# Row masks on VectorE, the gate's weights earlier in the load queue, early rows turned inside the last attention step, and w2 loaded in halves

## The chip, the cores and the metric

The kernel runs on one core of a Trainium2 chip. The metric is the device time of one execution in microseconds. Smaller is better.

A core has these engines: PE (TensorE, matrix products and transposes by a unit matrix), DVE (VectorE), ACT (ScalarE), POOL (GpSimd) and SP (SyncE, which here only starts transfers). Each takes its instructions in the order of the program, so one that waits holds up all that stand behind it on the same engine. Matrix products are written to PSUM, and DVE or ACT carry them on to SBUF.

## What is computed

A recurrent attention, then a mixture of experts on its output, all in float32.

```python
# retention: B=4, H=8 heads, S=768 steps, D=64; gamma depends on the head
for t in range(S):
    state = gamma * state + outer(k[:, :, t], v[:, :, t])
    y[:, :, t] = (q[:, :, t] @ state) / sqrt(D)
x = y.transpose(0, 2, 1, 3).reshape(3072, 512)      # one row per token
# experts: E=8, hidden width F=1024
logits = x @ w_gate                                  # (3072, 8)
expert = argmax(logits, axis=1)
gate   = softmax(logits)[row, expert]
for e in range(E):
    rows = (expert == e)
    out[rows] = gate[rows] * (relu(x[rows] @ w1[e]) @ w2[e])
```

## The kernel before, in words

**Attention.** The 768 positions are cut into 6 chunks of 128, and the work into 12 steps (STEPS). A step handles one chunk of two of the four batches. The order of instructions on every engine is the order of the program: a manual schedule covers all engines from line 738 on. A step s does the following.

- SP starts the loads of k and v three steps ahead, in odd steps those of q too (lines 762 to 766). SP's queue is one line: the loads, then the stores of finished rows (`store`, line 586), then the weights of the first expert. The loads of steps 0 to 2 are started before the loop (lines 727 to 737), and the load of the gate's weights `wg` follows them (line 739).
- POOL scales q and v by the decay (`scale_q`, `scale_v`, lines 473 and 481).
- PE makes the scores (`scores`, 513), whose causal mask DVE applies (line 523, tile `am`); adds the part that comes from the state (`with_state`, 534); multiplies the output of the step before by the gate's weights (`logits`, 595, tile `parts`); turns the next step's k and, in odd steps, q (`turn_k`, `turn_q`, tiles `trk` and `trq`); transposes the logits back (`logits_of`, 606); makes the next state (`next_state`, 544, tile `new`); and makes the output inside the chunk (`within`, 562, tile `y`), in two halves of the heads. ACT and DVE copy `y` to the tile `xT`.
- DVE turns `xT` to rows (`to_rows`, 580, tile `xg`), and SP stores them in device memory (`x_d`).

PSUM is handed out by tags: four banks "sc" (scores, `parts`, early products `hp`), two "tr" (`trk`, `new`, `rk`, `found`, `tre`), two "y". A tile waits until the bank it takes over has been read out.

**Routing.** `place(i)` (line 616) is a generator that is advanced in pieces. It places the tokens of steps 0 to 4 (i = 0), 5 to 8 (i = 1) and 9 to 11 (i = 2). Its pieces: the one-hot choice of an expert and the gate (627 to 652; POOL splits the gate in three bfloat16 parts, `told`, for i > 0); the rank of each token within its expert by small products `rk` (654 to 667); a mask `here` per tile of 128 tokens, which says in which row a token goes (`find`, 679 to 682: one instruction per tile, on DVE for i = 0 and on POOL for i > 0); the values `val` (692); the product `found` of both (699), and its addition to `inv`, the table from places to tokens (705). For i = 1 the rows of the first 256 tokens of experts 0 and 1 are then fetched from `x_d` by indirect transfers that POOL starts (`gather`, 709). A table `WHEN` (755) says at which points of steps 5 to 10 a piece is advanced: "p" is ahead of `logits`, "a" after the stores, "b" after `next_state`, "r" ahead of `within`, "c" after it.

**The early job.** After the last step, expert 0's first 256 rows (EARLY) are computed while the last tokens are placed: `xe` (821) brings the fetched rows into head order, PE turns them (`tre`, 833) to `xTa`, and eight rounds of `layer1` (tile `hp`, 843) make the hidden layer `hTa`. Between the rounds stand the pieces of `place(2)`: `rk` after round 1, `found` and `inv` after round 4. The second layer is done by `pair` (345) with seven half-size products instead of eight. They need sums of quarters of w2 (`halves_of_w`, 263, tiles `we`) and of the hidden layer (`halves_of_h`, 252, tiles `he`). Lines 850 to 872 set the order: `sources` (from places to tokens), gathers, gates, `arms` (sizes of the experts), the four `we` (0, 1, 3 on DVE, 2 on POOL), the four `he`, then `pair`, the turning of the late rows on DVE (213), and `targets` (187: eight small DVE instructions, which give the rows of the output).

**The eight jobs.** Then each expert has one job (from line 984) of two layers, with the rest of expert 0 first. DVE turns the rows of the next job, POOL makes the sums of the weights, SP loads weights two jobs ahead.

Of the kernel before, what the change touches and what calls it, by code (L numbers as in the profile page):

```python
# [53 lines left out]
def kernel(  # L54
# [99 lines left out]
            nc.sync.dma_start(w1t[:, :, :, part], w1v[:, ds(e, 1), :, part])  # L154
        return w1t

    def weights2(pool, e):
        w2t = pool.tile([P, 1, FT, DM], F32, tag="w2t", name="w2t")
        nc.sync.dma_start(w2t, w2v[:, ds(e, 1), :, :])
        return w2t  # L160

    def weights(pool, e):
# [89 lines left out]
    def halves_of_h(hT, hs, others=nc.vector):  # L252


        hs = [h.rearrange("p (f t) -> p f t", f=FH) for h in hs]
        a11, a12, a21, a22 = (hT[:, ts(j, FH), ts(i, P)] for i in range(2) for j in range(2))
        nc.vector.tensor_tensor(out=hs[0], in0=a21, in1=a22, op=ALU.add)
        nc.vector.tensor_tensor(out=hs[1], in0=hs[0], in1=a11, op=ALU.subtract)
        others.tensor_tensor(out=hs[3], in0=a12, in1=hs[1], op=ALU.subtract)
        others.tensor_tensor(out=hs[2], in0=a11, in1=a21, op=ALU.subtract)  # L260
        return hs

    def halves_of_w(w2t, ws, which=range(4), by=nc.vector):
# [176 lines left out]
    with ExitStack() as actx:  # L440
# [87 lines left out]
        def outputs():  # L528
            return [ps("y", 2, "y").rearrange("p (b a t) -> p b a t", b=2, a=HB) for _ in range(2)]
# [29 lines left out]
            else:  # L559
                nc.vector.tensor_tensor(out=state[b1], in0=new, in1=old, op=ALU.add)  # L560

        def within(s, y, am):
            alone = 2 * where[s][0] + where[s][2] == 0
            x[s] = keep.tile([P, DT, 2, P], F32, tag="xT", name="xT", bufs=2)
            for half in range(2):
                for b in range(2):
                    vs = raw["vs", s, b]
                    for a in range(half * HB, (half + 1) * HB):
                        for j in ((1, 0) if half else (0, 1)):
                            nc.tensor.matmul(place_of(y, b, a, j), lhsT=vs[:, 2 * a + j, :], rhs=am[b][j][:, a, :],  # L570
                                             start=alone, stop=True, skip_group_check=True)
            nc.scalar.copy(out=x[s][:, 0:HB, :, :].rearrange("p a b t -> p b a t"), in_=y[0])
            for j in range(2):
                to, got = x[s][ts(j, D), HB:HP, :, :].rearrange("p a b t -> p b a t"), y[1][ts(1 - j, D), :, :, :]
                if j and s + 1 == STEPS:
                    nc.vector.tensor_copy(to, got)
                else:
                    nc.scalar.copy(out=to, in_=got)

        def to_rows(s):  # L580
            xg = x["g", s] = keep.tile([P, 2, Q, DT * L], F32, tag="xg", name="xg", bufs=3)
# [34 lines left out]
        def place(i):  # L616
# [61 lines left out]

            def find():
                for b in range(n):  # L680
                    by.tensor_scalar(out=here[:, b, :], in0=rrow, scalar1=prow[:, b : b + 1], scalar2=None,
                                     op0=ALU.is_equal)

            if i:
                find()
            else:
                yield
                tell()
                yield
# [4 lines left out]
                ap=[list(at_f.ap[0]), list(at_f.ap[1]), [0, 5], list(at_f.ap[2])]))  # L694
            if i == 0:
                yield
                find()
            yield
            found = ps("tr", 2, "found")[:, 0 : 5 * E * TC]
            for b in range(n):  # L700
# [22 lines left out]
        def load_all(nm, s):  # L723
            for b in range(2):
                load(nm, s, b)
# [2 lines left out]
        load("k", 0, 0)  # L728
        load("q", 0, 1)
        load("k", 0, 1)  # L730
        load_all("v", 0)
        load_all("k", 1)
        load_all("v", 1)
# [2 lines left out]
        load_all("k", 2)  # L736
        load_all("v", 2)
        ctx.enter_context(tc.manual_schedule(engines={PE, ACT, POOL, DVE, SP}))
        nc.sync.dma_start(wg[:, :, 0:E], w_gate.rearrange("(dt p) e -> p dt e", p=P))
        xTa = first.tile([P, DT, EARLY], F32, tag="xTa", name="xTa")  # L740
        xT1 = first.tile([P, DT, W], F32, tag="xT1", name="xT1")
        hTa = keep.tile([P, FT, EARLY], F32, tag="hTa", name="hTa")
# [8 lines left out]
        turn_k(0, 1)  # L751
        am.append(scores(0, 1))
        xe = keep.tile([P, HALF, DM], F32, tag="xe", name="xe")
        rest = iter(())
        WHEN = {5: "abc", 6: "ab", 7: "ab", 8: "pa", 9: "ar", 10: "pp"}

        def step(s, at):
            for _ in range(WHEN.get(s, "").count(at)):
# [2 lines left out]
        for s in range(STEPS):  # L761
            if s + 3 < STEPS:
                if s % 2:
                    load_all("q", s + 3)
                load_all("k", s + 3)
                load_all("v", s + 3)
            if s % 2 and s + 1 < STEPS:
                scale_q(s + 1, 1)
            if s + 1 < STEPS:
                for b in range(2):  # L770
                    scale_v(s + 1, b)
            if s % 2 == 0 and s + 2 < STEPS:
                scale_q(s + 2, 0)
            if s in (1, 2):
                nc.gpsimd.memset(xs2[s % 2], 0.0)
            if s:
                am = [scores(s, b) for b in range(2)]
            y = outputs()
            if where[s][0] or where[s][2]:
                with_state(s, y)  # L780

            def ahead():
                for b in range(2):
                    turn_k(s + 1, b)

            def ahead_q():
                if s % 2:
                    for b in range(2):
                        turn_q(s + 1, b)

            step(s, "p")
            if s:
                logit = logits(s - 1)
                if s + 1 < STEPS:
                    ahead()
                reduce = logits_of(s - 1, *logit)
                if s + 1 < STEPS:
                    ahead_q()
                to_rows(s - 1)
                reduce()  # L800
                store(s - 1)
                if s == NEXT[NR - 1]:
                    wa = [weights1(first, 0, 2)]
                if s + 1 == STEPS:
                    wa.append(weights2(first, 0))
                if s in NEXT:
                    rest = chain(rest, place(NEXT.index(s) - 1))
                step(s, "a")
            next_state(s)
            step(s, "b")  # L810
            if s == NEXT[NR - 1] + 1:
                pad_ranks(acc[:, NR - 1, 0:2])
            step(s, "r")
            within(s, y, am)
            if s == 0:
                ahead()
            step(s, "c")

        for t in range(HALF):
            copy = nc.scalar.copy if t else nc.vector.tensor_copy  # L820
            copy(out=xe[:, t, :].rearrange("p (a q l) -> p q a l", q=Q, l=L),
                 in_=xs2[0][:, t, :].rearrange("p (q a l) -> p q a l", q=Q, l=L))
        logit = logits(STEPS - 1)
# [6 lines left out]
        for t in range(HALF):  # L830
            tr = ps("tr", 2, "tre").rearrange("p (a t) -> p a t", a=DT)
            for dt in range(DT):
                nc.tensor.transpose(tr[:, dt, :], xe[:, t, ts(dt, P)], ident)
            if t:
                nc.scalar.copy(out=xTa[:, :, ts(t, P)], in_=tr)
            else:
                nc.vector.tensor_copy(xTa[:, :, ts(t, P)], tr)
        logits_of(STEPS - 1, *logit)()
        next(rest)
        to_rows(STEPS - 1)  # L840
        store(STEPS - 1)
        for f in range(FT):
            layer1(EARLY, xTa, wa[0], hTa, f, (("sc", 4),))
            if f == 1:
                next(rest)
                ne = count()
            if f == 4:
                next(rest)
                next(rest, None)
        src, far = sources(inv, "")  # L850
# [229 lines left out]
```

## Time and profile before

| | |
|---|---|
| median of three runs (and the three) | 470.91 us (471.14, 470.91, 466.03) |
| the profiled execution's own time | 469.96 us |
| its span, first to last instruction | 468.2 us, so 1.76 us lie around it |
| attention steps, early job, jobs | from 0 to 129, to 165, to the end (us in the span) |
| mean granted TensorE clock | 0.978 |
| bytes moved | 72.77 MB, mean 155 GB/s |

How to read the profile. The page gives busy time per engine, then the span in 40 slices. The chain of waits follows the work that ended last back to what released it. A timeline line has start and length in us, the engine, the line of the code, the operation, the tiles (out<-in) and a count; the brackets hold the idle time ahead of it and what ended it. "SPq" is the queue that starts transfers: a long entry there is an instruction that could not hand over its transfer sooner. "PEld" is the loading of a matrix operand, which overlaps the products. Windows give busy time per engine in a stretch, the granted TensorE clock (1.00 is full speed), the share of the transfer engines' time and the rate.

### The profile page before, as it was taken

The numbers are of one execution on the slowest core, as the hardware profiler recorded it, in microseconds if no ns is written. First come the engines' busy times: TensorE is split into PE (matmuls) and PEld (weight loads), VectorE is DVE, ScalarE is ACT, GpSimd is POOL, SyncE is SP. The second block draws the span as 40 slices with busy tenths as digits, with TensorE's granted clock in tenths as the row PEclk, the third lists the DMA queues.
The fourth block names the chain that finished last, engine by engine and source line by source line (L and its number), as shares of the span: only waits on it lengthen the run. The fifth ranks groups of instructions, "written<-read, shape, count | busy, mean of one in ns | idle before, by whom it ended". The sixth has DMA issues, their size and how long they took to land.

```text
span 468.2 us, 9505 instructions
## 1 busy us (share of the span) xinstructions
PE 437.6 (93%) x3595; PEld 358.8 (77%) x3595; DVE 277.4 (59%) x571; ACT 125.2 (27%) x284; POOL 258.0 (55%) x217
## 2 busy tenths in 40 slices
PE   7779999998887999999999999999989999999992
PEld 5668888786675884558987995898889599699772
DVE  4416469957558693942676567358756748744410
ACT  2334563552322020221231122114212212212310
POOL 4548535518246137819833891886389189179311
PEclk9979999998999799999999999999999999999998
DMA  8999999996671079705804441380472416001001
GB/s 200 226 238 208 236 228 227 227 228 207 165 237 41 3 256 383 293 4 208 285 3 183 156 168 50 138 299 22 182 227 91 174 44 223 5 6 63 4 28 49
DMA packets 94457, 72.77 MB, mean 155 GB/s; under 512 B 53883, under 2 KB 78459, under 8 KB 94337
## 3 DMA queue, kind: packets, MB, share of 16 engines
q1 hardware_dynamic: 89072, 58.74, 43.9%
q0 software_dynamic: 5120, 12.60, 7.6%
q8 instruction: 48, 0.79, 0.7%
q14 instruction: 73, 0.59, 0.4%
q10 hardware_dynamic: 144, 0.05, 0.0%
HBM read 60.88 MB, written 14.68 MB: 161 GB/s over the span
## 4 chain that ended last, share of the span: by engine, by line
PE 78%; DVE 7%; DMA 4%; SPq 3%; issue 2%; POOL 2%; ACT 1%; POOLq 0%; DVEq 0%; ACTq 0%
PE p L307 24%; PE p L353 18%; PE p L240 13%; PE p L227 5%; PE y L570 3%; PE sc L521 3%; DMA q<-in_q_dram 3%; DVE xT L213 2%; SPq L470 2%; PE new L554 2%; PE trk L489 2%; PE hp L227 2%; PE yp L353 1%; PE y L541 1%; PE parts L600 1%
## 5 line engine op out<-in xcount | busy, mean ns | idle before, releaser
L240 PE MATMUL p<-w2t,hT 128*8 128x128 f32 (+6 forms) x496 | 66.7, 362 | 0.0
L240 PEld LDWEIGHTS p<-w2t,hT 128*8 128x8 f32 (+6 forms) x496 | 32.2, 122 | 30.2 <-issue 26.7
L213 DVE STREAM_TRANSPOSE xT<-xs 32x512 f32<-32x512 f32 x64 | 44.9, 702 | 6.3 <-issue 5.2
L398 POOL DMA_INDIRECT out_dram<-o,dst x30 | 29.9, 995 | 28.2 <-ACT o L248 11.8
L483 POOL TENSOR_TENSOR vs<-v,dec 128x512 f32<-128x512 f32 x23 | 23.6, 1046 | 38.3 <-PE y L570 33.9
L523 DVE TENSOR_TENSOR am<-sc,causal 128x512 f32<-128x512 f32 x48 | 29.9, 681 | 21.6 <-PE sc L521 21.6
L1039 POOL COPY turn_of<-t 128x1 f32<-128x1 f32 x6 | 1.1, 184 | 73.6 <-DVE t L293 73.6
L213 DVE STREAM_TRANSPOSE xTs<-xs 32x512 f32<-32x512 f32 x48 | 33.7, 702 | 11.9 <-issue 11.1
L353 PE MATMUL p<-ws,hs 128*128 128x256 f32 x168 | 37.4, 379 | 0.0
L170 POOL DMA_INDIRECT xs<-x_d,src x28 | 28.5, 1016 | 14.3 <-issue 7.9
L307 PE MATMUL p<-t,s 128*128 128x196 f32 (+5 forms) x192 | 35.8, 329 | 0.0
L307 PE MATMUL p<-t,w1t 128*128 128x196 f32 (+5 forms) x192 | 35.8, 329 | 0.0
L311 DVE TENSOR_TENSOR hT<-p,q 128x196 f32<-128x196 f32 (+5 forms) x72 | 23.8, 359 | 19.4 <-PE p L307 18.5
L353 PEld LDWEIGHTS p<-ws,hs 128*128 128x128 f32 x168 | 31.9, 190 | 4.3
L269 POOL TENSOR_TENSOR ws<-w2t,ws 128x1024 f32<-128x1024 f32 x14 | 33.1, 2363 | 0.5
L269 POOL TENSOR_TENSOR ws<-w2t 128x1024 f32<-128x1024 f32 x14 | 33.1, 2364 | 0.1
L307 PEld LDWEIGHTS p<-t,s 128*128 128x128 f32 x192 | 32.4, 190 | 0.0
L307 PEld LDWEIGHTS p<-t,w1t 128*128 128x128 f32 x192 | 32.4, 190 | 0.0
L359 DVE SCALAR_TENSOR_TENSOR o<-p,gate,q 128x256 f32<-128x256 f32 x21 | 10.1, 483 | 30.9 <-PE p L353 30.4
L521 PE MATMUL sc<-qT,kT 64*128 64x128 f32 x384 | 25.6, 280 | 2.5 <-ACT kT L508 2.3
L478 POOL TENSOR_TENSOR qs<-q,dec 128x512 f32<-128x512 f32 x22 | 22.4, 1045 | 9.6 <-DMA q<-in_q_dram 9.6
L311 DVE TENSOR_TENSOR q<-p,q 128x196 f32<-128x196 f32 (+5 forms) x48 | 16.3, 360 | 19.0 <-PE p L307 14.4
(211 smaller groups left out, 842.9 us busy)
## 6 DMA issues: line engine op xcount, KB each, us to landing
w2t<-in_moe_w_dram SPq DMA_DIRECT2D x8, 2048.0 KB
w1t<-in_moe_w_dram SPq DMA_DIRECT2D x7, 2048.0 KB, 8.2
k<-in_k_dram SPq DMA_DIRECT2D x24, 256.0 KB, 5.2
v<-in_v_dram SPq DMA_DIRECT2D x24, 256.0 KB, 4.7
x_d<-xg SPq DMA_DIRECT2D x48, 128.0 KB, 3.7
q<-in_q_dram SPq DMA_DIRECT2D x11, 512.0 KB, 6.7
w1t<-in_moe_w_dram SPq DMA_DIRECT2D x2, 1024.0 KB
q<-in_q_dram SPq DMA_DIRECT2D x2, 256.0 KB, 3.5
```

Of the source, the lines that this page charges most:

```text
L170: nc.gpsimd.indirect_dma_start(out=xs[:, t, :], out_offset=None, in_=x_d[0:rows, :], in_offset=bass.IndirectOffsetOnAxis(ap=idx[:, t : t + ...
L213: nc.vector.transpose(xT[ts(g, L), :, 0 : n * P].rearrange("p a (t r i) -> p r t a i", r=Q, i=L)[:, r, :, :, :], xs[ts(r, L), tiles[0] : t ...
L227: nc.tensor.matmul(hp, lhsT=w1t[:, 0, dt, ts(f, P)], rhs=xT[:, dt, 0:n], start=(dt == 0), stop=(dt == DT - 1))
L240: nc.tensor.matmul(y[j * z : j * z + m, 0:c], lhsT=hT[:, f, t * P + r0 : t * P + r0 + m], rhs=w2t[:, 0, f, ts(j, c)], start=(i == 0), stop ...
L269: by.tensor_tensor(out=ws[i], in0=sums[i][0], in1=sums[i][1], op=ALU.subtract)
L307: nc.tensor.matmul(rows(y), lhsT=a(d, f), rhs=b(d), start=start and d == 0, stop=d == 1, skip_group_check=True)
L311: nc.vector.tensor_tensor(out=to, in0=rows(y), in1=rows(plus), op=ALU.add)
L353: nc.tensor.matmul(y, lhsT=a[:, f, :], rhs=b[:, f, :], start=start and f == 0, stop=f == FH - 1, skip_group_check=True)
L398: done = nc.gpsimd.indirect_dma_start(out=out[:, :], out_offset=bass.IndirectOffsetOnAxis(ap=idx[:, t : t + 1], axis=0), in_=o[:, t, :], i ...
L483: by.tensor_tensor(out=vs, in0=raw.pop(("v", s, b)), op=ALU.mult, in1=inner(dec[:, ts(NC + 2 * where[s][0] + where[s][2], H)], D))
L521: nc.tensor.matmul(sc[j][:, a, :], lhsT=kT[r, a, :], rhs=qT[r, a, :], start=True, stop=True)
L523: nc.vector.tensor_tensor(out=am[j], in0=sc[j], in1=middle(causal[:, :], HP), op=ALU.mult)
```

## The change

Six edits are made at once:

1. `find` always runs on DVE, after `val`; so the masks `here` of `place(1)` (8 instructions) and `place(2)` (6) go from POOL to DVE.
2. The load of `wg` stands ahead of the loads of v in SP's queue. In the built program it comes right after the first of the two loads of v for step 0.
3. In `WHEN`, step 8 has "pp" in place of "pa": the addition to `inv` of `place(0)` stands ahead of `logits`, the turning of k and `to_rows`.
4. In the last step, `logits` of the step before stands ahead of `with_state`; ACT makes both `xe`; PE turns the early rows between the two halves of `within`, and the copy of the first half of `y` follows that half (in every step). The copy of the second half is on ACT alone.
5. The logits of the last step come after round 0 of `layer1`, their reduction, the first piece of `place(2)`, `to_rows` and the stores after round 1, `rk` after round 3, `count` after round 4, `found` and `inv` after round 6. w2 of expert 0 is loaded in two halves of 1 MB: the first where the whole was, the second behind the last stores.
6. `targets` of the main table is done ahead of the sums `we`; the fourth `we` stands after the `he`; in `halves_of_h` the third sum is made before the fourth (in the jobs too).

```diff
-    def weights2(pool, e):
-        w2t = pool.tile([P, 1, FT, DM], F32, tag="w2t", name="w2t")
-        nc.sync.dma_start(w2t, w2v[:, ds(e, 1), :, :])
+    def weights2(pool, e, part=range(FT), w2t=None):
+        if w2t is None:
+            w2t = pool.tile([P, 1, FT, DM], F32, tag="w2t", name="w2t")
+        part = slice(part.start, part.stop)
+        nc.sync.dma_start(w2t[:, :, part, :], w2v[:, ds(e, 1), part, :])
...
+        others.tensor_tensor(out=hs[2], in0=a11, in1=a21, op=ALU.subtract)
         others.tensor_tensor(out=hs[3], in0=a12, in1=hs[1], op=ALU.subtract)
-        others.tensor_tensor(out=hs[2], in0=a11, in1=a21, op=ALU.subtract)
...
-        def within(s, y, am):
+        def within(s, y, am, between=lambda: None):
...
             for half in range(2):
+                if half:
+                    between()
...
-            nc.scalar.copy(out=x[s][:, 0:HB, :, :].rearrange("p a b t -> p b a t"), in_=y[0])
+                if not half:
+                    nc.scalar.copy(out=x[s][:, 0:HB, :, :].rearrange("p a b t -> p b a t"), in_=y[0])
...
-                if j and s + 1 == STEPS:
-                    nc.vector.tensor_copy(to, got)
-                else:
-                    nc.scalar.copy(out=to, in_=got)
+                nc.scalar.copy(out=to, in_=got)
...
-                    by.tensor_scalar(out=here[:, b, :], in0=rrow, scalar1=prow[:, b : b + 1], scalar2=None,
+                    nc.vector.tensor_scalar(out=here[:, b, :], in0=rrow, scalar1=prow[:, b : b + 1], scalar2=None,
                                      op0=ALU.is_equal)
-            if i:
-                find()
-            else:
+            if i == 0:
...
             if i == 0:
                 yield
-                find()
+            find()
...
         load("k", 0, 1)
+        nc.sync.dma_start(wg[:, :, 0:E], w_gate.rearrange("(dt p) e -> p dt e", p=P))
         load_all("v", 0)
...
-        nc.sync.dma_start(wg[:, :, 0:E], w_gate.rearrange("(dt p) e -> p dt e", p=P))
...
+        def early_rows():
+            for t in range(HALF):
+                copy = nc.scalar.copy if t else nc.vector.tensor_copy
+                tr = ps("tr", 2, "tre").rearrange("p (a t) -> p a t", a=DT)
+                for dt in range(DT):
+                    nc.tensor.transpose(tr[:, dt, :], xe[:, t, ts(dt, P)], ident)
+                copy(out=xTa[:, :, ts(t, P)], in_=tr)
...
-        WHEN = {5: "abc", 6: "ab", 7: "ab", 8: "pa", 9: "ar", 10: "pp"}
+        WHEN = {5: "abc", 6: "ab", 7: "ab", 8: "pp", 9: "ar", 10: "pp"}
...
             y = outputs()
+            if s + 1 == STEPS:
+                logit = logits(s - 1)
             if where[s][0] or where[s][2]:
                 with_state(s, y)
...
+                if s + 1 == STEPS:
+                    for t in range(HALF):
+                        nc.scalar.copy(out=xe[:, t, :].rearrange("p (a q l) -> p q a l", q=Q, l=L),
+                                       in_=xs2[0][:, t, :].rearrange("p (q a l) -> p q a l", q=Q, l=L))
                 reduce = logits_of(s - 1, *logit)
...
-                    wa.append(weights2(first, 0))
+                    wa.append(weights2(first, 0, range(FT // 2)))
...
-            within(s, y, am)
+            within(s, y, am, early_rows if s + 1 == STEPS else lambda: None)
...
         for f in range(FT):
             layer1(EARLY, xTa, wa[0], hTa, f, (("sc", 4),))
+            if f == 0:
+                logit = logits(STEPS - 1)
             if f == 1:
+                logits_of(STEPS - 1, *logit)()
                 next(rest)
+                to_rows(STEPS - 1)
+                store(STEPS - 1)
+                weights2(first, 0, range(FT // 2, FT), wa[1])
+            if f == 3:
+                next(rest)
+            if f == 4:
                 ne = count()
-            if f == 4:
+            if f == 6:
                 next(rest)
                 next(rest, None)
...
         arm, over = arms(ne)
+        dst = targets(inv, far, "")
         halves_of_w(wa[1], we, [0, 1])
         halves_of_w(wa[1], we, [2], nc.gpsimd)
+        S = halves_of_h(hTa, [att.tile([P, FH * P], F32, tag="k", name="he", bufs=8) for _ in range(4)], nc.gpsimd)
         T = halves_of_w(wa[1], we, [3])
-        S = halves_of_h(hTa, [att.tile([P, FH * P], F32, tag="k", name="he", bufs=8) for _ in range(4)], nc.gpsimd)
...
         turn(xs2[1], xT1, range(TC))
-        dst = targets(inv, far, "")
```

More of the change, by code (lines that the diff above doesn't have):

```diff
@@ L792 @@
             if s:
-                logit = logits(s - 1)
                 if s + 1 < STEPS:
+                    logit = logits(s - 1)
                     ahead()
+                if s + 1 == STEPS:
+                    for t in range(HALF):
+                        nc.scalar.copy(out=xe[:, t, :].rearrange("p (a q l) -> p q a l", q=Q, l=L),
+                                       in_=xs2[0][:, t, :].rearrange("p (q a l) -> p q a l", q=Q, l=L))
                 reduce = logits_of(s - 1, *logit)
@@ L817 @@
             step(s, "c")
[L819 to L823, printed above, removed]
         rest = place(NR - 1)
@@ L827 @@
               for tag, bufs in [("q", 4)] * 4]
[L830 to L841, printed above, removed]
         for f in range(FT):
             layer1(EARLY, xTa, wa[0], hTa, f, (("sc", 4),))
+            if f == 0:
+                logit = logits(STEPS - 1)
             if f == 1:
+                logits_of(STEPS - 1, *logit)()
                 next(rest)
+                to_rows(STEPS - 1)
[4 more added lines that the diff above has]
+            if f == 4:
                 ne = count()
-            if f == 4:
+            if f == 6:
                 next(rest)
```

## The prediction

> **What bounds the kernel now.** I read the page first, then what PE waited for, then the chain of waits, then timelines around each break.
>
> ```profile
> PE 437.6 (93%) x3595; PEld 358.8 (77%) x3595; DVE 277.4 (59%) x571; ACT 125.2 (27%) x284; POOL 258.0 (55%) x217
> ...
> PEclk9979999998999799999999999999999999999998
> DMA  8999999996671079705804441380472416001001
> ```
>
> PE is the bound nearly everywhere, and from 180 us on (the jobs) it has hardly a gap. The change must earn its time before that. There PEclk has three dips (slices of 11.7 us), and the transfer engines are full until about 105 us. What PE waited for up to 180 us, longest total first (total, times, longest):
>
> ```profile
> PE parts L600 <- DMA wg<-in_moe_w_gate_dram: 4.6, 1, 4.6
> PE yp L353 <- DVE he L258: 3.5, 1, 3.5
> ...
> PE found L701 <- POOL here L681: 2.0, 6, 0.3
> ```
>
> The chain (start, length) has the same three places:
>
> ```profile
> 20.44 1.64 POOL qs L478 x2
> ...
> 22.75 3.71 DMA wg<-in_moe_w_gate_dram
> 26.47 0.14 issue
> 26.60 1.08 PE parts L600 x8
> 27.68 1.90 PE trk L489 x8
> 29.58 0.43 PE parts L609 x2
> 30.01 2.48 PE trq L489 x16
> 32.49 1.08 PE new L554 x32
> ```
>
> PE stood from 22.0 to 26.6 for the gate's weights. What follows is slow as well: the clock is halved (windows of four us; PEclk is third from the right).
>
> ```profile
> 24.00:28.00 4.00, 1.40 (x10) 0.61 (x11) 0.00 (x0) 0.26 (x1) 3.15 (x4) 0.57 1.04 217
> 28.00:32.00 4.00, 4.00 (x24) 4.00 (x23) 0.23 (x1) 2.26 (x5) 1.16 (x1) 0.58 1.10 239
> ```
>
> Two timeline lines matter for DVE and POOL together: an addition of two SBUF tiles on DVE that takes 0.69 us elsewhere took 2.83 us beside POOL's sum, and ended 0.55 us after it.
>
> ```profile
> 147.65 2.43 POOL L269 TENSOR_TENSOR we<-w2t 128x1024 f32<-128x1024 f32 x1
> 147.80 2.83 DVE L257 TENSOR_TENSOR he<-hTa 128x512 f32<-128x512 f32 x1
> ```
>
> [...] clock 0.50 from 24.6 to 31.3, 113.4 to 116.4 and 150.9 to 157.4 us, each after 2.6 to 4.4 us of little work. [...] k and v move in 256 B pieces; the trace has 229 GB/s here (40 to 104 us) and 390 GB/s for the experts' weights.
>
> **Part by part,** gains counted positive, in the base of the times above.
>
> *wg early.* Its transfer is issued 17 us sooner, so the stall goes. The loads behind it slip by its own slot: an SP entry of 1.00 us, but 16 KB; I take 0.5. PE is free at 21.97. Next it needs k (last issue ended 20.07) and POOL's fourth product of q, which ended at 24.48, now 24.98. At full clock `parts`, `trk`, `parts`, `trq` take 0.57+1.02+0.22+1.75 (rows of the step at 45 us). If only q holds, the last quarter of `trq` (0.44) follows at 24.98, and `new` starts at 25.5. If k lands 5 us after its issue ended (v's time to landing is 4.9), 25.1+0.22+1.75 gives about 27.5 with gaps. I take 26.4 against 32.41: **+6.0** (4.9 to 6.9).
>
> *Does it last to step 9?* The SP queue is never free until 105 us, so the loads keep their times; PE alone moves up. The narrow places: q of step 8 was scaled by 75.33 and is turned at 81.92; q of step 10 by 93.16, turned at 101.4; the last k of step 8 lands by about 74 (issue plus 4.6), turned at 81.1. Shifts of 6.0 to 7.2 leave 0.6 to 1.2 us. It lasts, barely.
>
> *Step 8, inv ahead.* `found` holds one of the two "tr" banks until `inv`, which ran at 93.48, behind `to_rows` and the logits; so the second `trk` waited 0.73 and `new` 0.60. Now `inv` follows `am` (end 91.38) and ends at 91.7: `trk` 91.75, `parts`, `new` at 92.65 instead of 93.84: **+1.2** (0 to 1.2).
>
> *Step 10, here on DVE.* Now POOL's eight masks (0.60 us apart, with a lock by `val` 5.65 in all) hold `found` until 112.53. On DVE one takes 0.24 us alone, 0.17 from start to start, as step 7's first ones did; 8 make 1.4. `val` ends at 108.1, masks at 109.5, then the four `am` that stand behind them on DVE; `parts` needs the first `am`'s bank: 110.25 instead of 112.46. The second `trk` waits for `inv` behind `am` (112.4). `new` starts at 113.25 and takes 1.15 instead of 1.84, [...]. `within` at 114.4 instead of 117.03: **+2.6**. The lower bound: POOL's two products for v of step 11 (1.04 each) stood behind the masks and now are free. If they fall on `val` and the masks, DVE loses 2.1 us, the clock falls, and the part gives -0.6. Their v is issued at 98.03 and 98.95 and lands at about 102.6 and 103.6; shifted by 7.2, the masks end at 102.3. So +2.6.
>
> *Last step.* From `within` of step 10 to that of step 11 is 7.7 us: scores 2.93, of which 0.87 is gaps, `with_state` 1.40, a wait of 0.55 for `lgT`. With `parts` ahead that wait is covered: 6.4: **+1.3** (0.4 to 1.9).
>
> *Early rows.* From `within` to the first `hp` now 5.7 us. Then: half 0.95, `tre` 1.1, half 0.9: 2.9: **+2.8**. It needs `xe` in time: ACT makes it during `with_state` if the gathered rows are there (rivals).
>
> *Given back before inv.* From first `hp` to the end of `inv`: 11.0 us now, five rounds of 1.8 plus 2. Afterwards seven rounds (12.6), `parts` 0.6, transposes 0.3, `rk` 0.3, `found` 0.6, `inv` 0.35: 14.8: **-3.8**. DVE's chain (masks ready 0.05 after round 5) and the second half of w2 (behind the stores; lands 4 us before it is needed) are hidden under these rounds. `place(2)`'s masks on DVE cost nothing: POOL ended them at 139.9, PE asked at 140.5.
>
> *From inv to he.* PE's stall of 3.5 us is on DVE: 9.92 us from `inv` to the second `he`. Out goes the fourth `we` (1.27), in come eight `targets` (1.45, 178.26 to 179.71). POOL's `we` still locks the first `he`; POOL's own `he` no longer waits for DVE's, so it may lock the second (1.26). Between 10.3 and 11.5: **-0.9** (-0.4 to -1.6).
>
> *The tail.* `targets` ended at 179.7; PE waited 0.55 for it before job 1. Job 0 ends at 179.13 and the turned rows at 178.23: **+0.5**.
>
> *Nothing:* the swapped order of sums in the jobs; both are ready before the third product, and if not, 0.69 us per job.
>
> Sum: 6.0+1.2+2.6+1.3+2.8-3.8-0.9+0.5 = +9.7. From the profiled execution (span 468.2, 1.76 around it, 469.96): span 458.5, **460.3 us**. The median of the runs shown is 0.95 higher.
>
> **Rivals.**
>
> *The loads take over* (0.20). Leads of 0.6 to 1.2 us rest on landing times that I could only bound. If k or q comes 3 us late, PE stops at `trk` or `trq` in steps 7 to 10: 3+0+1.5 for the first three parts, +4.4 in all: 465.6. For it: transfer share 0.9 to 1.1 throughout. Against: PE waited for no k in steps 2 to 11.
>
> *The lock and the clock* (0.14). v of step 11 lands early, [...] the third part is -0.6: 463.4. Decides whether the vs products start before the masks end.
>
> *More* (0.07). DVE is past its first `he` when POOL's `we` begins, and PE's rest before `yp` gets short enough for full clock: 24 products took 8.46 us where 24x0.237 = 5.7 would do. About +14: 456.
>
> *Slower* (0.05). PE's `tre` now stands inside the last step, and the second half of `within`, `hp` and all behind it queue there. It needs `xe`, that needs the gather, that needs step 8's stores to have landed, which SP's queue keeps at about 108.3 (issue to 104.94, plus 3.7). The second gather would start at 109.6; `tre` is due at 114.1. Each us of delay costs one; from a landing at 123.8 on the kernel is slower. The trace only shows that rows whose second issue began at 116.52 were there by 127.25; the same 10.7 gives 120.3. I put it at 471.5.
>
> *As forecast* (0.54).
>
> **How the numbers follow.** 2% is about what a measurement of this kernel can tell from no change; it is 461.5 us against the median. The forecast case spreads by some 1.5 us, so about 0.8 of it is past 2%, with the case "more" and a little of the lock's 0.52; slower by over 2% 0.04; within 0.44. The range 455.5 to 467.0 leaves out half of "slower" and the ends of the first and third rival. The forecast's own range is 458 to 463.
>
> **What would show it.** Right: no wait for wg, clock 1.00 from 24 to 32, `new` of step 1 at 26 to 27; no POOL masks; PE's gap before `parts` of step 10 under 2 us with clock 1.00 after it; first `hp` near 116; `inv` near 131; still a wait of `yp` for `he`, now longer than 3.5. Wrong: PE waits for k, q or qs between 35 and 105; `val` or `here` on DVE with lengths of 1 us or more; a wait of `tre` for `xe`; `found` late after round 6.

## The result, and the profile after

The changed kernel takes 463.75 us (median of 18 runs, 460.40 to 466.17), the kernel before 467.69 us (18 runs beside it, 464.38 to 472.94). The ratio is 0.991 with a 95% interval of 0.9884 to 0.9937: 4.2 us less, between 2.9 and 5.4. By 2% that counts as the same. The forecast was 460.3 with a range of 455.5 to 467.0. (The ratios leave out runs that lie over 1.5% above the fastest of their kernel, so they can differ from the ratio of two medians.)

The two profiled executions stand 9.5 us apart (span 468.2 and 458.7), nearly the forecast sum of 9.7. That agreement is partly luck: the profiled execution of the changed kernel is the fastest of its 18, and 1.65 of the 9.5 us arise behind the start of job 1, where the change has no term. Finding out how much is luck was the main work of the experiments. The page of the changed kernel has, for the busy row and the clock and transfer rows that the prediction showed of before:

```profile
PE 432.3 (94%) x3595; PEld 352.8 (77%) x3595; DVE 278.8 (61%) x583; ACT 126.1 (27%) x286; POOL 249.1 (54%) x203
...
PEclk9999999999995999999999999999999999999998
DMA  9999999999750099425614713281481524001001
```

The dips of PEclk in the third and the tenth slice are gone, and one is left at 140 us, where VectorE makes the `he`. What PE waited for up to 180 us (total, times, longest):

```profile
PE yp L355 <- DVE he L260: 4.9, 1, 4.9
...
PE yp L355 <- DVE bt L196: 2.0, 1, 2.0
...
PE rk L657 <- DVE ohs L636: 1.5, 1, 1.5
PE trk L491 <- DMA k<-in_k_dram: 1.4, 2, 0.9
```

`wg` has left the list, and `found <- POOL here` with it. In their place stand `rk` for DVE (0.2 before), `trk` for the landing of k and `yp` for `bt` (neither in the list of before). The last costs nothing: it ends at 136.7 us, and eight products later PE waits for `he` until 144.2 in any case. The wait for `he` has grown by 1.4. The chain (start, length) from 18 us on shows what holds PE where `wg` did:

```profile
17.71 5.98 DMA k<-in_k_dram
...
23.73 0.66 PE trk L491 x4
...
24.61 1.75 PE trq L491 x16
26.35 1.08 PE new L556 x32
```

and the windows over the same eight microseconds, which ran at 0.57 and 0.58 of the clock before, are now at full clock (PEclk is third from the right):

```profile
24.00:28.00 4.00, 4.00 (x68) 3.83 (x68) 0.74 (x2) 2.79 (x5) 3.14 (x3) 1.00 1.08 231
28.00:32.00 4.00, 4.00 (x65) 3.28 (x62) 1.87 (x4) 1.85 (x4) 2.42 (x3) 1.00 0.96 235
```

The next table follows the path through the timelines. Later experiments left the code up to some point untouched, so that one piece of code was traced several times; the columns "all" give those traces, the first one included (`tail_only`, which stands in two rows of before, differs there in the order of the copies of `y`).

| start of (us) | before | before, all | changed | changed, all |
|---|---|---|---|---|
| `new`, step 1 | 32.42 | 30.9 to 32.4 (3) | 26.29 | 26.2 to 26.7 (11) |
| `new`, step 8 | 93.84 | 92.3 to 93.8 (3) | 86.47 | 86.4 to 88.9 (8) |
| `new`, step 10 | 115.15 | 114.3 to 115.2 (3) | 106.14 | 106.1 to 109.3 (8) |
| first `hp` | 130.44 | 129.7, 130.4 | 118.75 | 118.5 to 121.6 (8) |
| end of last `inv` | 141.44 | 140.7, 141.4 | 133.24 | 133.2 to 135.9 (5) |
| job 0 | 164.98 | 162.1, 165.0 | 157.29 | 157.3 to 159.9 (4) |
| job 1 | 179.68 | 179.7 | 171.78 | 171.8, 174.7 |
| end | 468.2 | 468.2 | 458.7 | 458.7, 464.5 |

The traced execution of the changed kernel is near the early end of its kind at every mark, and that of the kernel before near the late end. By the means of these few traces the gain is 10.0 us at the first `hp` (130.1 against 120.1) and 5.3 at job 0 (163.5 against 158.2), where the profiled pair has 11.7 and 7.7.

### The profile page after: what moved, and what is told of

Read it like the earlier page. It is cut to its first block, busy times and chain, and to the rows that moved or that the text cites. A ratio compares the mean times of both kernels' runs of the same rounds, so it can differ in the third digit from the quotient of the medians.

```text
span 458.7 us, 9508 instructions
## 1 busy us (share of the span) xinstructions
PE 432.3 (94%) x3595; PEld 352.8 (77%) x3595; DVE 278.8 (61%) x583; ACT 126.1 (27%) x286; POOL 249.1 (54%) x203
## 4 chain that ended last, share of the span: by engine, by line
PE 82%; DVE 7%; SPq 4%; DMA 3%; issue 2%; ACT 1%; POOL 0%; POOLq 0%; DVEq 0%; ACTq 0%
PE p L309 24%; PE p L355 18%; PE p L242 15%; PE p L229 6%; PE sc L523 3%; PE y L574 3%; PE hp L229 3%; SPq L472 2%; PE new L556 2%; PE trk L491 2%; PE y L543 2%; PE trq L491 2%; DMA xs<-x_d,src_e 1%; DMA k<-in_k_dram 1%; DVE xTa L215 1%
## 5 line engine op out<-in xcount | busy, mean ns | idle before, releaser
L242 PEld LDWEIGHTS p<-w2t,hT 128*8 128x8 f32 (+6 forms) x496 | 32.1, 122 | 31.0 <-issue 26.7
L309 PEld LDWEIGHTS p<-t,w1t 128*128 128x128 f32 x192 | 32.4, 190 | 0.7 <-DVE q L313 0.7
L309 PEld LDWEIGHTS p<-t,s 128*128 128x128 f32 x192 | 32.4, 190 | 0.0
```

What stands on the lines that cost most here:

```text
L242: nc.tensor.matmul(y[j * z : j * z + m, 0:c], lhsT=hT[:, f, t * P + r0 : t * P + r0 + m], rhs=w2t[:, 0, f, ts(j, c)], start=(i == 0), stop ...
L309: nc.tensor.matmul(rows(y), lhsT=a(d, f), rhs=b(d), start=start and d == 0, stop=d == 1, skip_group_check=True)
```

## The experiments

**The parts alone, and the change once more.** All four ran on one chip. The first edit is

```diff
         load("k", 0, 1)
+        nc.sync.dma_start(wg[:, :, 0:E], w_gate.rearrange("(dt p) e -> p dt e", p=P))
         load_all("v", 0)
```

with the later issue taken out; the second adds to it `8: "pp"` in `WHEN` and the masks on VectorE; the third is the changed kernel with exactly these three edits taken back; the fourth is unaltered.

> The kernel before with the gate's weights moved ahead of v and nothing else. Prices as forecast: 6.0 us less than before, and the lead is kept to the end. Loads take over: part of the lead is lost in steps 7 to 10 to landings of k, q and v in most executions, so that only 2 to 4 us are left in the median, whatever one trace shows. Tail to blame: as forecast, about 6.

> The kernel before with the three edits of the attention steps: gate's weights ahead of v, inv of step 8 ahead, masks on VectorE; the last step and the early job as before. Prices as forecast: 9.8 us less than before. Loads take over: 4 to 5 us less, and the changed kernel as a whole is no worse than this one. Tail to blame: 8 to 10 us less than before, so 4 to 6 us faster than the changed kernel.

> The changed kernel with its three edits of the attention steps taken back: only the last step and the early job are the new ones. Prices as forecast: within 0.5 us of before (+1.3+2.8-3.8-0.9+0.5 = -0.1). Loads take over: the same, about 0. Tail to blame: 4 to 6 us slower than before.

> The changed kernel once more, unaltered, for a second trace and for times on the same chip as its parts. If its one trace (span 458.7) was a lucky execution, this one lies nearer 462, and the stretch that is longer tells what varies; if the trace was typical and the jobs or what lies around the span vary, the milestones up to job 0 repeat within 0.5 us.

| kernel | median us (runs) | ratio to before, 95% interval | in us |
|---|---|---|---|
| before | 469.89 (29) | | |
| `wg_alone` | 464.74 (6) | 0.990 (0.9867 to 0.9933) | -4.7 (-6.2 to -3.1) |
| `front_only` | 463.70 (6) | 0.9885 (0.9842 to 0.9928) | -5.4 (-7.4 to -3.4) |
| `tail_only` | 471.58 (19) | 1.0049 (1.0029 to 1.007) | +2.3 (+1.4 to +3.3) |
| `after_again` | 466.20 (11) | 0.9924 (0.989 to 0.9957) | -3.6 (-5.2 to -2.0) |

The parts add up (-5.4 + 2.3 = -3.1 us, beside -3.6 and -4.2 for the whole). Nearly all of the gain is the gate's weights; the two other edits of the attention steps bring under 1 us beside it, which is within the intervals; and the half of the change that was forecast at -0.1 to +0.1 costs about 2. So neither "prices as forecast" nor either rival holds alone: the front falls short by some 4 of 9.8, the tail by 2.

The second trace of the unaltered change lost 1.1 us against the first up to job 0, and 4.7 behind it. Of that, 3.5 stand at the entry of job 1, a wait longer by 1.9 and slower products:

```profile
174.70 22.95 PE L229 MATMUL p<-xT,w1t 128*128 128x392 f32 x64 [2.12 <-DMA w2t<-in_moe_w_dram]
```

PE waited 2.12 us (0.26 in the first trace), and these 64 products took 22.95 us instead of 21.31. The line names the landing of w2 as releaser. Taken at its word it gave the theory of the handover, which the next four runs test beside two undone edits and a new order for VectorE.

**Scatter held back; targets late; masks on GpSimd; sums first.** On another chip, before 468.29 us (35 runs). The edits, in this order:

```diff
+                nc.gpsimd.tensor_copy(turn_of, w2s[1][:, 0, 0, 0:1])
+                scatter(oa, early_to, range(HALF))
                 gather(xs2[0], cols[2][0], range(TC))
```
```diff
-        dst = targets(inv, far, "")
         halves_of_w(wa[1], we, [0, 1])
...
         turn(xs2[1], xT1, range(TC))
+        dst = targets(inv, far, "")
```
```diff
-                    nc.vector.tensor_scalar(out=here[:, b, :], in0=rrow, scalar1=prow[:, b : b + 1], scalar2=None,
+                    by.tensor_scalar(out=here[:, b, :], in0=rrow, scalar1=prow[:, b : b + 1], scalar2=None,
```
```diff
                 ne = count()
+                arm, over = arms(ne)
+                halves_of_w(wa[1], we, [0])
...
-        halves_of_w(wa[1], we, [2], nc.gpsimd)
-        S = halves_of_h(hTa, [att.tile([P, FH * P], F32, tag="k", name="he", bufs=8) for _ in range(4)], nc.gpsimd)
+        S = halves_of_h(hTa, [att.tile([P, FH * P], F32, tag="k", name="he", bufs=8) for _ in range(4)], between=(
+            lambda: halves_of_w(wa[1], we, [1]), lambda: halves_of_w(wa[1], we, [2]), lambda: None))
         T = halves_of_w(wa[1], we, [3])
```

The third also puts the masks back to where GpSimd issued them; in the fourth the callables of `between` run behind `he1` and behind `he2`, and the targets follow the early pair.

> The changed kernel, with GpSimd's scatter of the early rows and the gathers behind it held back until w2 of job 1 has landed (a one-column copy of that tile stands ahead of them). Theory of the handover: job 1 waits at its entry for the landing of all its weights, some 13 to 15 us after their issue, which shares the transfer engines with the scatter and the gathers; PE's lead is lost there in many executions, with a halved clock behind it. Then this is 2 to 4 us faster than the changed kernel (6 to 8 under before), and PE enters job 1 within 0.3 us of the end of job 0. Rival, jobs: the loss lies in jobs 2 to 5 and this is the same as the changed kernel, 3.8 us under before.

> The changed kernel with the eight targets back at the end of the early job, where they stood before. Prices as forecast: 0.4 us faster than the changed kernel (the second he 0.9 us sooner, 0.5 lost again at job 1). Theory of the handover: moving them ahead cost about 1.4 us at the second he and won nothing at job 1, which waits for its weights anyway: 1 to 1.5 us faster than the changed kernel. Rival, jobs: no difference.

> The changed kernel with the row masks of the second and third place on GpSimd again. Prices as forecast: 2.6 us slower than the changed kernel (step 10 takes 3.9 us more between within of step 9 and of step 10 by the two traces), 1.2 under before. Loads take over: q, k and v of steps 10 and 11 hold PE anyway, and the masks are worth under 1 us.

> The changed kernel with VectorE's work of the early job in another order: arm and the first we in its 2.0 us of rest ahead of found, then he0, he1, the second we, he2, the third we, he3, the fourth we, all on VectorE, with the targets behind the early pair. The second he is due at about 136.5 instead of 144.1 us (last round of hp at 134.65, its relu 0.4, two sums of 0.7), the first wait of yp falls from 4.9 to under 1 us, the clock stays full, and job 0 starts at 150.5 to 152 instead of 157.3. Theory of the handover: the weights of job 1 are issued at the end of the pair, so they move with it and 5 to 6 us are won to the end. Rival: the late rows, gathered at 134 to 139 us and turned by VectorE, become the bound, and under 3 us are won.

| kernel | median us (runs) | ratio to before, 95% interval | in us |
|---|---|---|---|
| `scatter_late` | 473.57 (6) | 1.0124 (1.0082 to 1.0165) | +5.8 (+3.8 to +7.7) |
| `targets_late` | 465.70 (14) | 0.9892 (0.9857 to 0.9926) | -5.1 (-6.7 to -3.5) |
| `masks_pool` | 465.55 (22) | 0.9944 (0.9922 to 0.9966) | -2.6 (-3.7 to -1.6) |
| `sums_first` | 457.34 (6) | 0.980 (0.975 to 0.9849) | -9.4 (-11.7 to -7.1) |

*Scatter held back* failed as an improvement: the gathers behind the scatter came 13 us later against the start of job 0, VectorE turned their rows from 192.8 instead of 178.1 us, its own work of job 1 stood behind that, and PE waited 2.9 us for it in layer 2; the eight products behind the wait took 3.75 us, the eight at 212.8 ahead of it 1.89. It still bears on the question. With w1 and w2 alone in the transfer engines, GpSimd's copy of its column ran when it had landed, and PE had begun job 1 before:

```profile
174.80 21.30 PE L229 MATMUL p<-xT,w1t 128*128 128x392 f32 x64 [0.66 <-DVE xT L215]
```
```profile
175.18 0.19 POOL L1035 COPY turn_of<-w2t 128x1 f32<-128x1 f32 x1 [12.48 <-DMA w2t<-in_moe_w_dram]
```

The two starts are 0.4 us apart, so this alone would leave room. But in the first trace of the change only about 4.5 MB had been moved when job 1 began (the windows from 158 to 171.8 us), where w1, w2 and the early rows make 4.7 (the last number is GB/s):

```profile
158.00:171.80 13.80, 13.54 (x77) 9.10 (x76) 12.25 (x25) 3.16 (x11) 7.03 (x8) 1.00 0.91 325
```

The packets settle it. Counted from the issue of w1, the queue of the weights has moved the 4.19 MB of w1 and w2 by 174.4 us both in the first trace of the change and in `hint_after`, a run described below. Job 1's first product starts at 171.8 us in the one and at 177.0 in the other. So job 1 does not wait for w2. What it waits for is in the instruction records: PE's branches. (Start and length in us; each job is a branch into one of several arms, by its row count.)

```
kernel         way out of job 0   entry of job 1   it ends   job 1's first product
before         172.62  0.63       174.36  4.64     179.00    179.68
after          165.01  0.67       166.78  4.42     171.20    171.78
after_again    166.06  2.17       169.35  4.76     174.11    174.70
targets_late   169.12  2.48       172.65  4.31     176.96    177.54
sums_first     157.67  0.71       159.43  4.55     163.98    164.75
hint_before    169.78  6.31       177.14  4.11     181.25    181.93
hint_after     165.10  5.76       171.98  4.43     176.41    177.00
```

In every trace job 1 starts 0.6 to 0.8 us behind the end of that branch, whichever releaser the profile names (targets, w2, turned rows, "issue"). Between the two stand only the next hint and four or five semaphore instructions. In twelve traces each of these takes 0.05 us, in `scatter_late` and `sums_first` one takes 0.16 and 0.18. So once the branch is over, PE has nothing left to wait for but these tenths. During each of these entries one packet of 16 KB starts on an instruction queue (in the kernel before at 176.6, inside 174.4 to 179.0). Over all 14 traces from 145 us on, 72 of PE's branches took longer than 2.34 us, and one such packet starts within each of them but one; within the 180 shorter ones none starts. The trace does not say for which engine a packet is: the long branches and the packets go together, and that a branch waits for its packet is not shown. The entries of later jobs vary between executions of one code: that of job 3 took 0.3 us in the first trace of the change and 2.5 in the second.

*Targets late.* Its trace shows what the targets cost ahead of the sums: from the end of `inv` to the end of the second `he` it takes 6.4 us, in the change 10.8.

```profile
140.81 0.68 DVE L259 TENSOR_TENSOR he<-hTa 128x512 f32<-128x512 f32 x1
141.52 0.69 DVE L260 TENSOR_TENSOR he<-he,hTa 128x512 f32<-128x512 f32 x1
```

The same two sums in the changed kernel:

```profile
139.58 2.83 DVE L259 TENSOR_TENSOR he<-hTa 128x512 f32<-128x512 f32 x1
142.44 1.63 DVE L260 TENSOR_TENSOR he<-he,hTa 128x512 f32<-128x512 f32 x1
```
```profile
139.38 2.49 POOL L271 TENSOR_TENSOR we<-w2t 128x1024 f32<-128x1024 f32 x1
141.82 1.71 POOL L261 TENSOR_TENSOR he<-hTa 128x512 f32<-128x512 f32 x1
```

Eight operations of 1.5 us in all pushed both sums beside GpSimd's, where they took 4.5 us instead of 1.4. In that trace the 4.4 us did not reach the end: the branch into job 0 took 3.4 us and PE stood 2.7. By the ratio, which keeps 9 of the 14 runs, the move back is worth 0.9 to 1.5 us, with overlapping intervals; by the two medians the kernel is only 2.6 us under before. So no gain over the change is shown.

*Masks on GpSimd* is 1.0 to 1.6 us slower than the change, less than the forecast 2.6, with overlapping intervals again.

*Sums first* is the fastest. VectorE's order, as its timeline has it:

```profile
131.64 1.22 DVE L273 TENSOR_TENSOR we<-w2t 128x1024 f32<-128x1024 f32 x1
132.77 0.31 DVE L707 TENSOR_TENSOR inv<-inv,found 128x160 f32<-128x160 f32 x1
134.82 0.69 DVE L259 TENSOR_TENSOR he<-hTa 128x512 f32<-128x512 f32 x1 [0.26 <-ACT hTa L231]
135.55 0.69 DVE L260 TENSOR_TENSOR he<-he,hTa 128x512 f32<-128x512 f32 x1
136.16 1.22 DVE L273 TENSOR_TENSOR we<-w2t,we 128x1024 f32<-128x1024 f32 x1
```

The second `he` ends at 136.2 instead of 144.1, each sum takes its own 0.7 us, and PE's wait falls from 4.9 to 1.4, with PEclk at 1.00 from 136 to 160 us, where the change has 0.73, 0.50 and 0.50 up to 148 (its last row starts the products of job 0):

```profile
137.52 5.42 PE L357 MATMUL yp<-we,he 128*128 128x256 f32 x24 [1.43 <-DVE we L273]
149.95 7.36 PE L229 MATMUL p<-xTa,w1t 128*128 128x104 f32 x64 [0.39 <-DVE xTa L215]
```

Job 0 starts at 149.95, half a microsecond ahead of the range written down (150.5 to 152), and not at 157.3. Alone, this run's interval reaches to either side of 2%; the repetition below is clearly past it. The run undoes several things at once (no sum on GpSimd, targets late, one sum ahead of `found`), and what each is worth was not separated.

**The hint.** PE's branch target of job 1 is named ahead by a hint, at the start of job 0's layer 2. Three of the last four runs give it after the third round of layer 1 instead (the lines not shown take the later one out), and the fourth repeats `sums_first`:

```diff
                     for f in range(FT):
                         layer1(n, xT, w1s[e], hT, f)
+                        if e == 0 and f == 2:
+                            hint()
```

> The kernel before, with the hint that names PE's and ScalarE's branch target of job 1 given after the third round of layer 1 of job 0 instead of at its layer 2. In all ten traces so far PE starts job 1 0.5 to 0.7 us after a branch of 4.3 to 4.8 us in its instruction stream has ended, whatever else is ready, and the hint stands only 3.7 us ahead of that branch. Theory of the branch: [...] the branch falls under 1.5 us, job 1 starts within 0.2 us of the end of job 0 (now 0.55), and the kernel is 0.5 us faster. Rival, landing of weights or targets: the branch ends early and PE still waits till the same time, no gain. Rival, [...] whose branch then takes 2 to 3 us: 1 to 3 us slower.

> The changed kernel with the same earlier hint. Theory of the branch: what its executions lose at the entry of job 1 (0.3 us in the first trace, 2.1 and 1.65 for a halved clock in the second) is gone; the median falls by 1 to 2 us, to 5 to 6 under before, and the times lie closer together. Rivals as for the kernel before: no gain, or 1 to 3 us slower.

> The kernel with VectorE's sums first, with the same earlier hint. Theory of the branch: 0.5 to 2 us under sums_again of the same chip, 12 us under before. Rivals: the same time, or 1 to 3 us slower.

> The kernel with VectorE's sums first once more, unaltered, for a second trace and for times beside sums_hint. It repeats 10 to 11 us under before, with the second he at 136 to 139 us, and its branches at the entries of jobs 2 to 6 differ from those of the first trace (0.3 or 1.5 to 3.7 us each) without any change in the code.

| kernel | median us (runs) | ratio to before, 95% interval | in us |
|---|---|---|---|
| before | 469.42 (32) | | |
| `hint_before` | 476.65 (6) | 1.0165 (1.0127 to 1.0204) | +7.7 (+6.0 to +9.6) |
| `hint_after` | 472.48 (22) | 1.0057 (1.0035 to 1.0079) | +2.7 (+1.6 to +3.7) |
| `sums_hint` | 465.72 (11) | 0.9926 (0.9898 to 0.9953) | -3.5 (-4.8 to -2.2) |
| `sums_again` | 457.97 (6) | 0.976 (0.9722 to 0.9798) | -11.3 (-13.1 to -9.5) |

My remedy was wrong and its rival right: the new hint costs 6 to 8 us in all three. The table of branches has why. The way out of job 0, which takes 0.6 to 2.5 us in the eleven other traces, takes 5.7 to 6.3, and the entry of job 1 stays at 4.1 to 4.6. In the changed kernel with the hint that is (the view ends after 63 of the 64 products, which take 23.71 us in all)

```profile
177.00 23.38 PE L229 MATMUL p<-xT,w1t 128*128 128x392 f32 x63 [5.38 <-DMA w2t<-in_moe_w_dram]
```

5.1 us of wait more than the first trace of the change had, and 2.4 more for job 1, whose first five products took 3.61 us (1.7 at the pace of 64 in 21.31): 7.5. That is the clearest sign that the branch sets the start of job 1: the edit moves nothing but the hint. In these three traces the next packet of 16 KB starts 9.8 to 10.4 us behind the moved hint, inside the way out; in the eleven others it starts 0.2 to 2.1 us behind the hint. It is the way out of job 0 that grew, as the rival had it. What the second hint does to the first is not shown, and why the entry stays at 4.1 to 4.8 us whenever the hint is given is open; it was not tried further.

`sums_again` repeats the gain. Its branches into jobs 3 to 6 take 3.1, 1.5, 2.3 and 3.0 us, in the first trace of the same code 0.4, 0.4, 3.7 and 2.9, and its span is 3.5 us longer; 2.3 of them came before job 0.

## Why the prediction was partly right, step by step

The range held, the time was 3.4 us above the forecast one, and the cases beside the likeliest explain part of that.

- **The base.** The sum was made against one execution. In all these traces PE's clock is halved for 3.413 us or a whole multiple of it at a time, but for the stretch that the end of the kernel cuts off (6.83 us from 24.55, 3.41 at 113.29, 6.83 at 150.84 in the kernel before). The same wait is not followed by the same stretch each time: `hint_before`, the same code up to job 0, has 3.41 us at 26.02, 3.41 at 111.36 and none at 150, though PE waited the same 3.5 us for `he`. Its 24 products of `yp` took 6.3 us instead of 8.5, and job 0 came 2.9 us sooner (0.7 of that it had already at the first `hp`). A part of every saving that I priced with a halved clock was luck of that trace.
- **wg early, +6.0:** the mechanism is right, the size was off for that reason. 6.1 in the pair; 4.7 by the ratio of `wg_alone`. The two other traces of the old order have 3.4 us of half clock there instead of 6.8 and reach `new` of step 1 at 30.9 and 31.1 us. The next holder of PE is the landing of k, as the working had it.
- **Does it last to step 9:** the leads of 0.6 to 1.2 us were too thin in part of the executions. In eight traces `new` of step 7 starts between 77.7 and 80.2 us, up to 2.5 apart. In the latest of them, `sums_hint`, PE waited for the landing of k by 1.02 us at 59 and by 0.78 at 97 us (1.95 in all behind 24 us, 1.4 in `front_only`); in the first trace of the change it waited for none there. So the rival "loads take over" holds in part of the executions, with waits of up to 2 us, where the rival put its loss at 5.3.
- **Step 8, +1.2:** right. From `new` of step 7 to that of step 8 it is 10.08 us in the old order and 8.69 to 8.70 in the new one: 1.4.
- **Step 10, +2.6:** too high by about half, by the ratio of `masks_pool`. From `rk` to `new` of step 10 it is 11.7 to 12.4 us in the old code, 10.2 with the weights moved alone (no half clock at 113 us), and 8.5 or 9.3 with the masks on VectorE. The two values are what the rival called the lock: in five of these eight traces GpSimd's first product for v of step 11 falls on the masks, and the eight take 2.18 us instead of 1.39. It costs 0.8 us, where the rival had 3.2. `new`, forecast at 1.15 us, took 1.15 in the changed kernel, with PEclk at 1.00 from 103 to 110 us. A trace of each kind, the first one the changed kernel's own, the second `after_again`:

```profile
101.27 1.39 DVE L683 TENSOR_SCALAR here<-rrow,prow 128x128 bf16<-128x128 bf16 x8
```
```profile
101.79 2.18 DVE L683 TENSOR_SCALAR here<-rrow,prow 128x128 bf16<-128x128 bf16 x8
```

- **A slowdown of VectorE beside GpSimd that I had not looked for** stands ahead of it. GpSimd's products for v of step 10, waiting for their landing now that PE is ahead, fall on `place(1)`: `dl` and `top` took 0.80 and 0.93 us for 0.22 and 0.20, and PE waited 1.5 for `ohs` (the new line in the list of waits). VectorE and GpSimd of the changed kernel there:

```profile
95.07 0.80 DVE L630 TENSOR_TENSOR dl<-lg,mx 128x64 f32<-128x64 f32 x1
95.90 0.93 DVE L632 TENSOR_SCALAR top<-dl 128x64 f32<-128x64 f32 x1
```
```profile
94.74 2.04 POOL L485 TENSOR_TENSOR vs<-v,dec 128x512 f32<-128x512 f32 x2 [2.04 <-DMA v<-in_v_dram]
```

- **Last step, +1.3:** failed. From `within` of step 10 to that of step 11 it is 7.7 us again in the pair, and 7.5 to 8.5 in the eight traces. The wait of 0.55 for `lgT` is gone, but the move made another. `parts` takes its bank from the four of "sc", which the scores of the step have just filled, so it needs the first `am` of its own step. In the old order `with_state` (1.5 us) stood between scores and `parts` and covered that; the forecast named this dependence for step 10 and left it out here. In seven of the eight traces PE waits 0.7 to 2.1 us for it. In `after_again`:

```profile
113.91 2.48 DVE L525 TENSOR_TENSOR am<-sc,causal 128x512 f32<-128x512 f32 x4 [3.75 <-PE sc L523]
114.75 0.64 PE L602 MATMUL parts<-xT,wg 128*32 128x256 f32 x8 [2.13 <-DVE am L525]
```

The first trace of the change is the exception: it lists no such wait, but `with_state` takes 2.7 instead of 1.5 there, with gaps that the trace puts down to nothing. Why `am` starts 3.4 us behind the first product of the scores in `after_again`, where it is 2.2 in the kernel before, is open.
- **Early rows, +2.8:** 2.0 in the pair, 2.3 to 2.6 in the nine other traces of the split `within`. In the pair ScalarE waited 0.71 and 0.49 for the gathered rows, PE 0.39 for `xe`.
- **Given back, -3.8, and inv to he, -0.9:** -3.5 and -0.9. But the second sum hides what `targets_late` showed: the eight targets ahead of the sums cost not their 1.45 us but 4.4, since VectorE's two sums then run beside GpSimd's and take 4.5 us instead of 1.4.
- **The tail, +0.5:** failed. I read "PE waited 0.55 for `far`" as a wait that moving the targets would take away. In all traces the branch into job 1 ends last there: behind it no semaphore instruction took over 0.18 us. With the targets gone PE waited 0.26 us in the changed kernel's trace and 0.81 in that of `tail_only`. The first lines of job 1, before and after:

```profile
179.68 21.30 PE L227 MATMUL p<-xT,w1t 128*128 128x392 f32 x64 [0.55 <-DVE far L198]
```
```profile
171.78 21.31 PE L229 MATMUL p<-xT,w1t 128*128 128x392 f32 x64 [0.26 <-issue]
```

Together: the front brought some 5 us instead of 9.8, and the tail cost about 2 us where I had it at nothing (-0.1). The five terms of the tail come to 0.0, +2.0, -3.5, -0.9 and +0.2 in the pair, which is -2.2 and near the ratio of `tail_only`. By these marks the last step's 1.3, the early rows' 0.8 and 0.3 at job 1 are what is missing. The targets' cost is not part of it: it lies within the -0.9, which held. The trace of `tail_only` itself divides the loss in another way (early rows +2.6, job 1 -0.3), so the shares are not settled, and how much of the 2.3 is a less fortunate branch into the jobs no trace tells.

## What to carry to other kernels

Before pricing a stall from one trace, ask what part of it is a halved clock, for that part differs between executions (6.8 us around 28 us in the kernel before, 3.4 in `hint_before`, the same code up to there); two traces of one code up to a common point show it at once. When an engine's idle time at the start of a branch is put down to several releasers in turn, read the branch itself: at job 1 it ended last every time, and the edit that cleared one of the named releasers won 0.3 us at most there. Before moving an instruction ahead of another, ask what the other one covered: `parts`, moved ahead of `with_state`, met the wait for its bank. Work that is moved out of a tail can cost more than its length if it pushes other work beside that of another engine (the targets' 1.45 us cost 4.4 at the second `he`, next to GpSimd's sums); give the slot of rest to what the longest wait needs, as `sums_first` did for 2.0 to 2.4% against the kernel before.

## What the hardware showed that I had not expected

- The entry of job 1 takes 4.1 to 4.8 us of PE's instruction stream in all 14 traces. With its hint 4.4 us sooner, 2.0 to 2.2 us behind the one given at the entry of job 0, the way out of job 0 took about 6 us instead of 0.6 to 2.5.
- The length of PE's branches goes with the instruction packets: all but one of the 72 longer than 2.34 us had one of 16 KB start within them, none of the 180 shorter ones had.
- The same branch in the same code took 0.4 us in one execution and 3.1 in another (the entry of job 3 in `sums_first` and `sums_again`), and the stretch from job 0 to the end took 301.4 us in one trace and 306.1 in another of one kernel, which is more than this change is worth.
